# One PSUM tile per bank of attention scores, row maxima taken bank by bank, and the routing polynomial moved to VectorE from the third routing on

## The chip, the cores and the metric

One core of one Trainium2 chip runs the whole kernel; the other cores of the chip are idle. The metric is the time of one execution in microseconds (us), measured on the device. The kernel before takes 931.32 us, the median of 3 runs (929.89 to 932.29).

Names: PE is TensorE (PEld its weight load), DVE is VectorE, ACT is ScalarE, POOL is GpSimd and SP is SyncE, which here only issues DMAs. PSUM is the matmul result memory; it has 8 banks of 512 fp32 words per partition.

## The reference

Attention (batch 4, 8 heads, 768 positions, head dimension 64) in which a position sees the 96 positions up to itself and the first 8 of the sequence, with a linear distance bias; its output goes through a mixture of 8 experts, of which each of the 3072 tokens takes the best two by noisy logits.

```python
scores = scale * q @ k.T + bias;  scores = where(keep, scores, -1e9)
a = exp(scores - max(scores));  a = a / (sum(a) + 1e-9);  x = a @ v
noisy = x @ w_gate + log1p(exp(x @ w_noise)) * noise
top2 = argpartition(-noisy, 2)[:, :2]
top2_w = exp(l - max(l)) / (sum + 1e-9)          # l: the two noisy logits
for e in experts, k in range(2):                  # tokens whose k-th choice is e
    out[mask] += top2_w[mask, k, None] * (relu(x[mask] @ w1[e]) @ w2[e])
```

All matmuls of the experts are fp32, each done as three products of halves (hi*hi, lo*hi, hi*lo).

## The kernel before, in words

Each engine works through its own queue in the order in which the code issues instructions, with semaphore waits put in wherever two of them touch the same tile. No scheduler moves anything: the code order is the order.

**Attention** runs over 24 groups of 128 queries (`g`), two steps each, 48 steps `s` in all. A step handles two units `n` and `n+1`, where a unit is four score blocks laid out in one PSUM bank. The steps are software-pipelined. Step `s`, with `n = 2s`, issues in this order:

1. `trans(n)`: PE turns the probabilities of step `s` (L601, into `atb`);
2. `probs(n+2)`: ACT takes two exponentials of one bank (L572);
3. in odd steps `heads_out` (L632, ACT) and `gate_s2` (DVE); in even steps `gate_l2` (L216, ACT) and `gate_x2` (L203, DVE);
4. `evac(n)`: ACT copies the turned probabilities out of PSUM (L607);
5. `probs(n+3)`: ACT, two exponentials of the other bank; `total(n+2)`: POOL sums the probabilities (L582, L584); `total2(n-2)`: DVE (L589);
6. some *ticks* of the routing, then `product(n+4)`: PE writes the next two units' scores (L544) and biases (L550) into two of the three banks of `scb`, unit `n` into bank `n % 3`; then `top(n+4)`: DVE takes the maxima of both banks at once (L562) and scales them (L563);
7. `attend(n-2)` (L625), and the gate's matmuls (`gate_l` L211, `gate_x` L199 in odd steps, `gate_s` L220 in even ones).

In step `s`, `product(n+4)` fills banks `(n+4) % 3` and `(n+5) % 3`. The second of these is the bank that `probs(n+2)` reads in the same step; `probs(n+3)` reads the third bank, which `product(n+4)` doesn't touch. But `scb` is one tile of three banks.

**Routing** (`route(r)`) is a generator for each of five segments of groups, `SEG`. A tick advances every active routing by one step, and the routing with `r == CLOSE` (2) by two. It holds small DVE and ACT operations, a polynomial for log1p (L255 to L269) on POOL, the search for the two best (L276, L278, DVE), prefix sums by matmul (L308 to L312, PE), and two scatters a group into the table `tbl` in DRAM (L333, POOL). Routings 0 to 2 finish within attention; the first expert's first four tiles of tokens are gathered from their entries (L344, L159), and turned by PE (L176) into the banks of `scb`. Routing 3 ends, and routing 4 runs, while PE does the first expert's first matmuls (L851), by a fixed list of steps:

```python
steps_of = [10, 60], [0, 23, 0, 0, 100]
```

The routing's matmuls therefore stand in PE's queue between the first expert's matmuls. When routing 4 has written its entries, the rest of the table is read (L937) and the tokens of the other tiles are gathered.

**The experts** are 571 us of nearly gapless matmuls (L851, L884, L894).

Of the kernel before, what the change touches and what calls it, by code (L numbers as in the profile page):

```python
# [10 lines left out]
F32 = mybir.dt.float32  # L11
# [9 lines left out]
P = 128  # L21
# [9 lines left out]
def tile_local_global_attention_then_moe(  # L31
# [204 lines left out]
    def route(r):  # L236
# [17 lines left out]
        po_ = nc.gpsimd  # L254
        po_.tensor_mul(u, u, t)  # L255
        po_.tensor_mul(t, u, u)
        yield
        po_.tensor_scalar(p, t, SP_C[7], SP_C[6], op0=OP.mult, op1=OP.add)
        for j in range(5, -1, -1):
            po_.tensor_mul(p, p, t)  # L260
            po_.tensor_scalar(p, p, SP_C[j], None, op0=OP.add)  # L261
            if j % 2 == 0:
                yield
        po_.tensor_mul(p, p, u)
        po_.tensor_scalar(u, n, 0.0, None, op0=OP.max)
        yield
        po_.tensor_add(p, p, u)
        po_.tensor_mul(p, p, noise_s[:, a:z])
        po_.tensor_add(ny, p, l[:, :, :E])  # L269
        for _ in range(4):  # L270
            yield
# [83 lines left out]
    with ExitStack() as actx:  # L355
# [36 lines left out]
        if windowed:  # L392
# [67 lines left out]
            scb = ap.tile([P, 3, 512], F32, name="scb")  # L460
# [47 lines left out]
        def tick():  # L508
            beat[0] += 1
            active[:] = [(x, r) for x, r in active if next(x, 0) is None and (r != CLOSE or next(x, 0) is None)]  # L510
# [9 lines left out]
        def product(n):  # L520
# [5 lines left out]
            for x in range(2):  # L526
                SC[n + x] = scb[:, (n + x) % 3, :2 * w].rearrange("p (y w) -> p y w", y=2)
# [27 lines left out]
        def top(n):  # L555

            g, u, b, i = geo(n)
            w = WIN if i else P
            j = sorted([n % 3, (n + 1) % 3])
            ps = scb[:, j[0]:j[1] + 1:j[1] - j[0], :2 * w].rearrange("p x (y w) -> p x y w", y=2)  # L560
            t = aw.tile([P, 2, 2], F32, name="mx", bufs=4)
            nc.vector.tensor_reduce(t, ps[:, :, :, :P + NS] if i else ps, op=OP.max, axis=AX.X, negate=True)  # L562
            nc.vector.tensor_scalar(t, t, scale, None, op0=OP.mult)  # L563
            for x in range(2):
                MX[n + x] = t[:, j.index((n + x) % 3)]
# [174 lines left out]
        else:  # L740
# [36 lines left out]
            for s in range(NPR + 1):  # L777
# [18 lines left out]
                if s:  # L796
                    total2(n - 2)
                    if not odd:
                        sums(s // 2 - 1)
                if s + 2 < NPR:  # L800
                    ticks(3 if odd else 1)
# [14 lines left out]
                if s >= NPR - 1:  # L816
                    for t in (2 * (s - NPR + 1), 2 * (s - NPR + 1) + 1):
                        turn(0, t, scb[:, t % 3])
# [262 lines left out]
```

## Time and profile before

| | us |
|---|---|
| median of 3 runs | 931.32 |
| the profiled execution | 933.77 |
| its span, first to last instruction | 932.0 |
| attention, up to the last scores (269.92) | 270 |
| from there to the first gapless expert matmuls (361) | 91 |
| the experts after that | 571 |

| engine | busy us | share | instructions |
|---|---|---|---|
| PE | 781.2 | 84% | 7399 |
| DVE | 328.5 | 35% | 783 |
| ACT | 321.1 | 34% | 688 |
| POOL | 306.9 | 33% | 407 |

Engines work side by side, so busy times don't add up to the span. A share over the whole span mixes the attention, in which PE waits in every step, with the experts, in which it doesn't. The waits of a step have to be read from that step.

### The profile page before, as it was taken

To read this page: it belongs to the slowest core of one execution; us is meant where nothing else is said; L and a number is where in the kernel's file an instruction comes from. 1 tells how busy PE (TensorE), PEld (TensorE's weight loads), DVE (VectorE), ACT (ScalarE), POOL (GpSimd) and SP (SyncE) were. 2 spreads that over 40 slices of the span, in tenths; PEclk is the share of its full clock that TensorE was granted. 3 is DMA by queue.
4 is the path that set the end of the run, shared out by engine and by line. 5 is a ranking of instruction groups with operands and counts; after the bars stand their busy time and mean duration, and the time that the engine had idled before them with its cause. 6 is when DMAs were issued, how large, how long until landed. Compare 5 with 4: busy or idle time off the path is not lost.

```text
span 932.0 us, 17968 instructions
## 1 busy us (share of the span) xinstructions
PE 781.2 (84%) x7399; PEld 680.9 (73%) x7399; DVE 328.5 (35%) x783; ACT 321.1 (34%) x688; POOL 306.9 (33%) x407
## 2 busy tenths in 40 slices
PE   4566666565565398999999999999999999999995
PEld 3555555554554386989889899898898998988994
DVE  5343554444333241433234234224333323323400
ACT  2444454443432131333333233233333333333301
POOL 3222546646452755140231312313214124032013
PEclk9998998878896798999999999999999999999998
DMA  9158455443103275252533444435335344342014
GB/s 286 52 179 275 132 169 145 145 155 117 44 26 106 75 149 110 71 148 91 104 87 97 90 114 114 90 110 126 77 77 126 105 94 117 100 83 51 4 15 61
DMA packets 61253, 100.54 MB, mean 108 GB/s; under 512 B 11674, under 2 KB 20122, under 8 KB 61162
## 3 DMA queue, kind: packets, MB, share of 16 engines
q1 hardware_dynamic: 45930, 72.62, 25.0%
q0 software_dynamic: 15232, 26.68, 16.1%
q8 instruction: 60, 0.98, 0.4%
q14 instruction: 31, 0.25, 0.1%
HBM read 71.03 MB, written 28.24 MB: 107 GB/s over the span
## 4 chain that ended last, share of the span: by engine, by line
PE 50%; issue 22%; POOL 10%; ACT 8%; DVE 4%; DMA 3%; another core or an unknown queue 1%; POOLq 0%; ACTq 0%; DVEq 0%
PE av L884 10%; PE at L851 9%; PE sc L851 9%; PE av L894 7%; PE scb L544 4%; ACT a L572 4%; ACT at L607 3%; POOL out_dram L869 3%; PE otb L625 2%; PE atb L601 2%; DVE mx L562 2%; POOL tbl L333 2%; POOL xg L159 1%; DMA tbl<-ent,sli 1%; POOL p L261 1%
## 5 line engine op out<-in xcount | busy, mean ns | idle before, releaser
L544 PE MATMUL scb<-ks,qbuf 64*64 64x128 f32 (+1 forms) x1408 | 48.5, 283 | 102.9 <-ACT a L572 97.5
L869 POOL DMA_INDIRECT out_dram<-y,tba x28 | 44.4, 1587 | 257.3 <-ACT y L868 257.3
L544 PEld LDWEIGHTS scb<-ks,qbuf 64*64 64x64 f32 x1408 | 40.9, 155 | 114.7 <-ACT a L572 109.4
L572 ACT ACTIVATE a<-scb,mx 128x192 f32<-128x192 f32 (+1 forms) x192 | 68.7, 415 | 127.2 <-DVE mx L563 84.7
L884 PE MATMUL av<-w2h,hh 128*128 128x512 f32 x256 | 103.2, 403 | 0.0
L884 PE MATMUL av<-w2h,hl 128*128 128x512 f32 x256 | 102.0, 398 | 0.0
L884 PE MATMUL av<-w2l,hh 128*128 128x512 f32 x256 | 101.6, 397 | 0.0
L851 PE MATMUL at<-xh,w1h 128*128 128x512 f32 (+1 forms) x256 | 91.5, 357 | 1.5 <-DVE xl L179 1.5
L144 DVE TENSOR_TENSOR w1l<-raw,w1h 128x512 fp32r<-128x512 f32 x56 | 38.3, 689 | 148.1 <-ACT w1h L143 148.1
L851 PE MATMUL sc<-xh,w1h 128*128 128x512 f32 (+1 forms) x256 | 89.9, 351 | 0.0
L851 PE MATMUL at<-xh,w1l 128*128 128x512 f32 (+1 forms) x256 | 89.8, 351 | 0.0
L851 PE MATMUL at<-xl,w1h 128*128 128x512 f32 (+1 forms) x256 | 89.8, 351 | 0.0
L851 PE MATMUL sc<-xl,w1h 128*128 128x512 f32 (+1 forms) x256 | 88.4, 345 | 0.0
L851 PE MATMUL sc<-xh,w1l 128*128 128x512 f32 (+1 forms) x256 | 88.4, 345 | 0.0
L869 POOL DMA_INDIRECT out_dram<-y,tbb x24 | 38.1, 1589 | 148.6 <-ACT y L868 148.3
L894 PE MATMUL av<-hh,w2h 128*128 128x300 f32 x256 | 78.9, 308 | 0.0
L582 POOL TENSOR_TENSOR tot<-a 128x256 f32<-128x256 f32 x48 | 35.0, 730 | 129.1 <-ACT a L572 129.1
L894 PE MATMUL av<-hl,w2h 128*128 128x300 f32 x256 | 77.1, 301 | 0.0
L894 PE MATMUL av<-hh,w2l 128*128 128x300 f32 x256 | 77.0, 301 | 0.0
L562 DVE TENSOR_REDUCE mx<-scb 128x4 f32<-128x672 f32 (+1 forms) x48 | 39.8, 829 | 100.3 <-PE scb L550 98.5
L862 DVE SCALAR_TENSOR_TENSOR hl<-sc,hh 128x300 fp32r<-128x300 f32 (+1 forms) x62 | 35.8, 577 | 103.8 <-ACT hh L861 99.4
L861 ACT ACTIVATE hh<-sc 128x300 fp32r<-128x300 f32 (+1 forms) x62 | 31.4, 507 | 99.4 <-PE sc L851 98.2
(154 smaller groups left out, 1659.0 us busy)
## 6 DMA issues: line engine op xcount, KB each, us to landing
raw<-in_w SPq DMA_DIRECT2D x32, 1024.0 KB
out_dram<-zero SPq DMA_DIRECT2D x14, 512.0 KB
qbuf<-in_q SPq DMA_DIRECT2D x24, 256.0 KB
vs<-in_v SPq DMA_DIRECT2D x24, 256.0 KB
xd<-xr SPq DMA_DIRECT2D x24, 256.0 KB
ks<-in_k SPq DMA_DIRECT2D x8, 560.0 KB
vp<-in_vb SPq DMA_DIRECT2D x40, 80.0 KB
ks<-in_k SPq DMA_DIRECT2D x6, 432.0 KB
```

The costliest lines, as they stand in the source:

```text
L144: eng.tensor_sub(lo, t, hi.bitcast(F32))
L544: nc.tensor.matmul(SC[n + x][s * Q:(s + 1) * Q, y, c:c + wc], qs[b, j][r, 2 * i0 + s, u + y], m, start=y == 0 and full, stop=False, tile_p ...
L562: nc.vector.tensor_reduce(t, ps[:, :, :, :P + NS] if i else ps, op=OP.max, axis=AX.X, negate=True)
L572: nc.scalar.activation(A[n][:, y, :3 if i else 2, n % 2], ps[:, y].rearrange("p (c t) -> p c t", t=Q), AF.Exp, bias=mx[:, y:y + 1], scale= ...
L582: nc.gpsimd.tensor_add(t, a[:, :, 0], a[:, :, 1])
L607: nc.scalar.activation(AT[n][:, :, :m].rearrange("p y c t -> p y (c t)"), atb[:, :, :m * P], AF.Copy)
L851: nc.tensor.matmul(ps, w[:, k, fs], x[c][:, k], start=n == 0, stop=n == 3 * KC - 1)
L861: nc.scalar.activation(hh[c][:, f], ps, AF.Relu)
L862: nc.vector.scalar_tensor_tensor(hl[c][:, f], ps, 0.0, hh[c][:, f].bitcast(F32), op0=OP.max, op1=OP.subtract)
L869: ins = nc.gpsimd.indirect_dma_start(out=out, out_offset=bass.IndirectOffsetOnAxis(ap=r[:, 0:1], axis=0), in_=y, in_offset=None, bounds_ch ...
L884: nc.tensor.matmul(ps, x[0][:, f, cols], w[:, f], start=n == 0, stop=n == 3 * FC - 1)
L894: nc.tensor.matmul(ps, w[:, f, cols], x[1][:, f], start=n == 0, stop=n == 3 * FC - 1)
```

## The change

Three edits. The three banks of `scb` become three tiles, and `top` reduces each bank by an instruction of its own. The polynomial stays on POOL for routings 0 and 1, with a yield after every second operation instead of every sixth; from routing 2 on it is on DVE in 13 instructions, each with a yield. Ticks advance every routing from 2 on by two steps instead of only routing 2, and there are ticks in the last two steps too.

```diff
-        po_ = nc.gpsimd
-        po_.tensor_mul(u, u, t)
...
-            po_.tensor_scalar(p, p, SP_C[j], None, op0=OP.add)
-            if j % 2 == 0:
+        if r < CLOSE:
+            nc.gpsimd.tensor_mul(u, u, t)
...
+                nc.gpsimd.tensor_mul(p, p, t)
+                nc.gpsimd.tensor_scalar(p, p, SP_C[j], None, op0=OP.add)
                 yield
...
+        else:
+            nc.vector.tensor_mul(u, u, t)
+            yield
...
+            for j in range(6, 0, -1):
+                nc.vector.scalar_tensor_tensor(p, p, SP_C[j], t, op0=OP.add, op1=OP.mult)
+                yield
...
+            nc.vector.tensor_add(ny, p, l[:, :, :E])
             yield
...
-            scb = ap.tile([P, 3, 512], F32, name="scb")
+            scb = [ap.tile([P, 512], F32, name=f"sc{j}") for j in range(3)]
...
-            active[:] = [(x, r) for x, r in active if next(x, 0) is None and (r != CLOSE or next(x, 0) is None)]
+            active[:] = [(x, r) for x, r in active if next(x, 0) is None and (r < CLOSE or next(x, 0) is None)]
...
-                SC[n + x] = scb[:, (n + x) % 3, :2 * w].rearrange("p (y w) -> p y w", y=2)
+                SC[n + x] = scb[(n + x) % 3][:, :2 * w].rearrange("p (y w) -> p y w", y=2)
...
-            nc.vector.tensor_reduce(t, ps[:, :, :, :P + NS] if i else ps, op=OP.max, axis=AX.X, negate=True)
+            for x in range(2):
+                nc.vector.tensor_reduce(t[:, x], SC[n + x][:, :, :P + NS] if i else SC[n + x], op=OP.max, axis=AX.X,
+                                        negate=True)
...
+                ticks(4 if s + 2 >= NPR else 3 if odd else 1)
                 if s + 2 < NPR:
-                    ticks(3 if odd else 1)
...
-                        turn(0, t, scb[:, t % 3])
+                        turn(0, t, scb[t % 3])
```

The order in PE's queue within a step is the same; its waits are not. Before, in a step of the attention (L601 transposes, L544 scores, square brackets for the semaphores that an instruction waits on):

```order
L601 MATMUL atb<-ident,a_220 128x128 x6
L544 MATMUL scb<-ks,qbuf_110 64x128 [waits DMAHW7_49,DVE_49,Activation_49]
L544 MATMUL scb<-ks,qbuf_110 64x128 x3
L544 MATMUL scb<-ks,qbuf_110 64x40 x4
L544 MATMUL scb<-ks,qbuf_110 64x128 x4
```

The first score waits for ACT, and everything behind it in the queue with it. In the changed kernel, where L616 are the transposes, L561 the scores, and `sc_223` to `sc_225` the three banks:

```order
L616 MATMUL atb<-ident,a_221 128x128 [waits Activation_49]
L616 MATMUL atb<-ident,a_221 128x128 x2
L616 MATMUL atb<-ident,a_221 128x128 [waits Activation_49]
L616 MATMUL atb<-ident,a_221 128x128 x2
L561 MATMUL sc_223<-ks,qbuf_110 64x128
L561 MATMUL sc_224<-ks,qbuf_110 64x128 [waits DVE_49,Activation_49]
L561 MATMUL sc_223<-ks,qbuf_110 64x128
```

Before, the one wait on ACT stood ahead of both banks' scores and also covered the transposes of the next step. Now the transposes have waits of their own, the first bank's scores have none, and the second bank's have one, on the exponentials that read that bank.

On POOL, at the end of attention and the start of the experts, this stood before (L333 scatters, then routing 4's polynomial L255 to L269, then `hl`, the low half of an expert's activations, L859):

```order
L333 DMA tbl<-ent_4070,sli_4134 25600x2 x8
L255 TENSOR_TENSOR u_4160<-u_4160,t_4161 128x32
L256 TENSOR_TENSOR t_4161<-u_4160 128x32
...
L268 TENSOR_TENSOR p_4162<-p_4162,noise_s 128x32
L269 TENSOR_TENSOR ny_4163<-p_4162,LG 128x32
L859 TENSOR_TENSOR hl_4045<-h,hh_4043 128x512
L144 TENSOR_TENSOR w2l<-raw,w2h 128x512
L859 TENSOR_TENSOR hl_4045<-h,hh_4043 128x512 x2
L333 DMA tbl<-ent_4211,sli_4293 25600x2 x8
```

And now, with the scatters on L350 and `hl` on L874:

```order
L159 DMA xg<-xd,tb_88 128x512 x4
L350 DMA tbl<-ent_3950,sli_4023 25600x2 x7
L874 TENSOR_TENSOR hl_4143<-h,hh_4141 128x512
L144 TENSOR_TENSOR w2l<-raw,w2h 128x512
L350 DMA tbl<-ent_3950,sli_4023 25600x2
L874 TENSOR_TENSOR hl_4143<-h,hh_4141 128x512
L144 TENSOR_TENSOR w2l<-raw,w2h 128x512
L874 TENSOR_TENSOR hl_4143<-h,hh_4141 128x512 x2
L350 DMA tbl<-ent_4296,sli_4322 25600x2 x8
```

The polynomial is gone from POOL here, and seven of routing 3's eight scatters stand ahead of the first expert's `hl`.

On DVE, routing 4's polynomial now stands between the reciprocal and the search for the two best (L293, L295):

```order
L272 TENSOR_TENSOR u_4196<-u_4196,t_4197 128x32
L274 TENSOR_TENSOR t_4197<-u_4196 128x32
L276 TENSOR_SCALAR p_4198<-t_4197 128x32
L279 SCALAR_TENSOR_TENSOR p_4198<-p_4198,t_4197 128x32 x6
L281 SCALAR_TENSOR_TENSOR p_4198<-p_4198,u_4196 128x32
L283 SCALAR_TENSOR_TENSOR p_4198<-LG,p_4198 128x32
L285 TENSOR_TENSOR p_4198<-p_4198,noise_s 128x32
L287 TENSOR_TENSOR ny_4199<-p_4198,LG 128x32
L293 MAX m_4218<-ny_4199 128x8 x2
```

Before, the polynomial was twenty instructions on POOL, and DVE's queue went from the reciprocal (L252) straight to a wait for POOL.

## Rows read from the trace of the kernel before

**Rows 1.** The profile's page: busy time, and the span in 40 slices of 23.3 us (PE's busy tenths, PE's granted clock in tenths of full speed).

```profile
PE 781.2 (84%) x7399; PEld 680.9 (73%) x7399; DVE 328.5 (35%) x783; ACT 321.1 (34%) x688; POOL 306.9 (33%) x407
...
PE   4566666565565398999999999999999999999995
...
PEclk9998998878896798999999999999999999999998
```

**Rows 2.** Stretches of the span: length, busy us of each engine (instructions), granted clock, DMA share, GB/s. 14.02, 91.17 and 269.92 are the starts of the scores of units 4, 34 and 94, the last: 15 and 30 steps apart.

```profile
14.02:91.17 77.15, 48.00 (x1134) 40.29 (x1135) 32.19 (x84) 34.93 (x88) 19.33 (x34) 0.93 0.58 190
91.17:269.92 178.75, 108.38 (x2554) 92.53 (x2554) 80.03 (x277) 77.07 (x195) 94.18 (x156) 0.86 0.40 122
361.00:932.00 571.00, 559.73 (x3200) 498.11 (x3198) 179.24 (x304) 184.72 (x354) 139.19 (x104) 0.99 0.39 91
```

**Rows 3.** Who waited for whom between 20 and 276 us: us in total, times, longest.

```profile
PE scb L544 <- ACT a L572: 91.4, 44, 4.9
ACT a L572 <- DVE mx L563: 76.4, 30, 3.2
DVE m L276 <- POOL ny L269: 14.2, 3, 5.6
```

**Rows 4.** The timeline of one step with no routing in it: start, us, engine and line; in brackets the idle time before, and what ended it.

```profile
86.24 0.88 PE L544 MATMUL scb<-ks,qbuf 64*64 64x128 f32 x32 [1.58 <-ACT a L572]
...
87.40 0.86 DVE L562 TENSOR_REDUCE mx<-scb 128x4 f32<-128x672 f32 x1 [2.21 <-PE scb L550]
...
88.29 0.17 DVE L563 TENSOR_SCALAR mx<-mx 128x4 f32<-128x4 f32 x1
...
88.58 0.73 ACT L572 ACTIVATE a<-scb,mx 128x192 f32<-128x192 f32 x2 [2.39 <-DVE mx L563]
...
89.20 0.60 ACT L632 ACTIVATE ot<-otb 128x512 f32<-128x512 f32 x1
89.68 0.82 ACT L607 ACTIVATE at<-atb 128x768 f32<-128x768 f32 x1
90.37 0.75 ACT L572 ACTIVATE a<-scb,mx 128x192 f32<-128x192 f32 x2
91.17 1.52 PE L544 MATMUL scb<-ks,qbuf 64*64 64x128 f32 x32 [2.54 <-ACT a L572]
...
93.12 0.86 DVE L562 TENSOR_REDUCE mx<-scb 128x4 f32<-128x672 f32 x1 [3.74 <-PE scb L550]
...
95.15 0.82 PE L601 MATMUL atb<-ident,a 128*128 128x128 f32 x6
```

**Rows 5.** PE's part of an odd step at full clock, the longer of the two kinds, from the same view.

```profile
269.92 0.88 PE L544 MATMUL scb<-ks,qbuf 64*64 64x128 f32 x32 [1.58 <-ACT a L572]
...
272.42 0.82 PE L601 MATMUL atb<-ident,a 128*128 128x128 f32 x6
```

**Rows 6.** POOL up to 345 us, and two groups of DVE up to 360 us, by line and shape: busy us, mean ns, idle time before.

```profile
L333 POOL DMA_INDIRECT tbl<-ent,sli x48 | 48.7, 1016 | 13.0 <-issue 10.7 <-DVE m L276 0.9 <-DVE sli L328 0.3
L582 POOL TENSOR_TENSOR tot<-a 128x256 f32<-128x256 f32 x48 | 35.0, 730 | 129.1 <-ACT a L572 129.1
L584 POOL TENSOR_TENSOR tot<-tot,a 128x160 f32<-128x160 f32 x40 | 20.9, 522 | 3.1
...
L563 DVE TENSOR_SCALAR mx<-mx 128x4 f32<-128x4 f32 x48 | 11.2, 234 | 1.7
L562 DVE TENSOR_REDUCE mx<-scb 128x4 f32<-128x512 f32 x8 | 5.5, 692 | 15.6 <-PE scb L550 15.6
L244 DVE SCALAR_TENSOR_TENSOR u<-LG 128x40 f32<-128x40 f32 x2 | 0.3, 148 | 0.0
```

**Rows 7.** Two small DVE instructions, each with the POOL instruction that ran at that time, from the timelines of both engines.

```profile
129.89 1.27 POOL L144 TENSOR_TENSOR w1l<-raw,w1h 128x512 fp32r<-128x512 f32 x1
130.20 0.98 DVE L563 TENSOR_SCALAR mx<-mx 128x4 f32<-128x4 f32 x1
302.64 1.31 POOL L859 TENSOR_TENSOR hl<-h,hh 128x512 fp32r<-128x512 f32 x1 [17.36 <-ACT hh L858]
302.69 1.31 DVE L244 SCALAR_TENSOR_TENSOR u<-LG 128x32 f32<-128x32 f32 x1
```

**Rows 8.** After the last scores: the timelines of PE, POOL and DVE.

```profile
282.59 1.11 PE L176 MATMUL scb<-ident,xg 128*128 128x128 f32 x4 [5.42 <-DMA xg<-xd,tb]
285.19 1.08 PE L176 MATMUL scb<-ident,xg 128*128 128x128 f32 x4 [1.49 <-DVE xl L179]
292.61 1.11 PE L176 MATMUL scb<-ident,xg 128*128 128x128 f32 x4 [1.41 <-DVE xl L179]
305.26 0.35 DVE L252 RECIPROCAL t<-t 128x32 f32<-128x32 f32 x1
315.42 0.27 POOL L255 TENSOR_TENSOR u<-u,t 128x32 f32<-128x32 f32 x1
322.03 0.25 POOL L269 TENSOR_TENSOR ny<-p,LG 128x32 f32<-128x32 f32 x1
322.32 0.24 DVE L276 MAX8 m<-ny 128x8 f32<-128x8 f32 x2 [16.70 <-POOL ny L269]
324.12 0.20 PE L308 MATMUL lg<-ohs,upper 128*128 128x8 bf16 x2 [14.33 <-DVE ohs L294]
357.62 0.93 PE L176 MATMUL m<-ident,xg 100*128 100x100 f32 x4 [2.59 <-DMA xg<-xd,tbb]
```

More of the change, by code (lines that the diff above doesn't have):

```diff
@@ L253, in route @@
         yield
-        po_ = nc.gpsimd
-        po_.tensor_mul(u, u, t)
[L256 to L260, printed above, removed]
-            po_.tensor_scalar(p, p, SP_C[j], None, op0=OP.add)
-            if j % 2 == 0:
-                yield
[L264 to L270, printed above, removed]
+        if r < CLOSE:
+            nc.gpsimd.tensor_mul(u, u, t)
+            nc.gpsimd.tensor_mul(t, u, u)
+            yield
+            nc.gpsimd.tensor_scalar(p, t, SP_C[7], SP_C[6], op0=OP.mult, op1=OP.add)
+            for j in range(5, -1, -1):
+                nc.gpsimd.tensor_mul(p, p, t)
+                nc.gpsimd.tensor_scalar(p, p, SP_C[j], None, op0=OP.add)
+                yield
+            nc.gpsimd.tensor_mul(p, p, u)
+            nc.gpsimd.tensor_scalar(u, n, 0.0, None, op0=OP.max)
+            yield
+            nc.gpsimd.tensor_add(p, p, u)
+            nc.gpsimd.tensor_mul(p, p, noise_s[:, a:z])
+            nc.gpsimd.tensor_add(ny, p, l[:, :, :E])
+            for _ in range(3):
+                yield
+        else:
+            nc.vector.tensor_mul(u, u, t)
+            yield
+            nc.vector.tensor_mul(t, u, u)
+            yield
+            nc.vector.tensor_scalar(p, t, SP_C[7], None, op0=OP.mult)
+            yield
+            for j in range(6, 0, -1):
+                nc.vector.scalar_tensor_tensor(p, p, SP_C[j], t, op0=OP.add, op1=OP.mult)
+                yield
+            nc.vector.scalar_tensor_tensor(p, p, SP_C[0], u, op0=OP.add, op1=OP.mult)
+            yield
+            nc.vector.scalar_tensor_tensor(p, n, 0.0, p, op0=OP.max, op1=OP.add)
+            yield
+            nc.vector.tensor_mul(p, p, noise_s[:, a:z])
+            yield
+            nc.vector.tensor_add(ny, p, l[:, :, :E])
             yield
@@ L557, in top @@
             g, u, b, i = geo(n)
-            w = WIN if i else P
-            j = sorted([n % 3, (n + 1) % 3])
-            ps = scb[:, j[0]:j[1] + 1:j[1] - j[0], :2 * w].rearrange("p x (y w) -> p x y w", y=2)
             t = aw.tile([P, 2, 2], F32, name="mx", bufs=4)
-            nc.vector.tensor_reduce(t, ps[:, :, :, :P + NS] if i else ps, op=OP.max, axis=AX.X, negate=True)
+            for x in range(2):
+                nc.vector.tensor_reduce(t[:, x], SC[n + x][:, :, :P + NS] if i else SC[n + x], op=OP.max, axis=AX.X,
+                                        negate=True)
+                MX[n + x] = t[:, x]
             nc.vector.tensor_scalar(t, t, scale, None, op0=OP.mult)
-            for x in range(2):
-                MX[n + x] = t[:, j.index((n + x) % 3)]
         def probs(n):
```

## The prediction

> **What bounds the kernel now.** I read the page first [rows 1]: PE is busy 84% of the span, but its tenths stand at 5 to 6 in slices 2 to 12, the attention, and at 9 behind them. A table of stretches comes next [rows 2]: from 361 us to the end PE works 559.7 of 571 us at a granted clock of 0.99, so the experts are bound by PE's own work and the change leaves that alone. In the attention the busiest engine, PE, works 48.0 of 77.15 us and 108.4 of 178.75, so there something else sets the pace. The waits [rows 3] name a ring: PE's scores wait 91.4 us for ACT's exponentials, ACT waits 76.4 us for the scaled maxima, and the maxima wait for the scores. The timeline of one step [rows 4] shows it link by link. The exponentials `probs(n+2)` run 88.58 to 89.31, then ACT does `ot`, the evacuation and the other bank's exponentials `probs(n+3)` (90.37 to 91.12); .05 us later, at 91.17, PE starts the scores. Thus both pairs of exponentials, the evacuation and `ot` stand in series with scores, maxima and scale: 86.24 to 91.17, 4.93 us a step.
>
> Over long stretches a step takes 77.15 / 15 = 5.14 us up to 91.17 and 178.75 / 30 = 5.96 us from there to 269.92, where the routings run [rows 2]. The rest, 270 to 361, is a chain of gathers, turns and routing 4 with PE often idle [rows 8].
>
> **The change, part by part.** The sums are made against the profiled execution's 933.77 us; the median of the runs, 931.32, is 2.45 lower, and I take that off at the end.
>
> *Three tiles for the three banks.* The second bank's scores now wait only for `probs(n+2)`, the first pair of the step, and the first bank's for a pair of the step before. The ring becomes: pair .73, start .05; start of scores to start of maxima 87.40 - 86.24 = 1.16; maxima; 88.58 less the maxima's end at 88.26 = .32 for the scale and the way to ACT [rows 4]. The maxima are now two instructions. One of 672 columns takes .86 and one of 512 .69 [rows 6], so a column costs .17 / 160 us and one of 336 comes to about .50, two to 1.00 instead of .86. Sum: .78 + 1.16 + 1.00 + .32 = 3.26 us. What is late next is not far behind: PE's own part of an odd step is 272.42 + .82 - 269.92 = 3.3 us [rows 5], and ACT's is .73 + .60 + .82 + .75 = 2.9 [rows 4]. With a PE of 3.3 and a ring of 3.3 that meet only on average, and with the .2 by which the steps of before exceeded their clean ring (5.14 against 4.93), I take 3.8 us for the quiet steps; 3.35 and 4.3 are the ends, the latter since the scores can run at the lower clock, where the way from scores to maxima is 93.12 - 91.17 = 1.95 and not 1.16 [rows 4]. **Term A**: 77.15 - 15 x 3.8 = 20, from 27 down to 12. The data for it have to keep up: the stretch moves 190 GB/s at a DMA share of .58 [rows 2], which becomes .58 x 77.15 / 57 = .79. That is under full, and I charge nothing; without that cover the stretch can't be shorter than .58 x 77.15 = 45 us, below my 57.
>
> *The thirty steps with routings* have the same ring and more beside it. What lengthened them by .82 us (5.96 against 5.14) is the routings' work in the queues of DVE and ACT, POOL's work and a clock of 0.86 against 0.93 [rows 2]. That part doesn't shrink with the ring, and the routing work now falls into a shorter time. I add 1.0 to 3.5, the midpoint of the ring with its locks and the 3.8 above without its .2 or .3: 4.5 us a step. **Term B**: 178.75 - 30 x 4.5 = 44, with 3.75 (66) and 5.2 (23) as ends. POOL keeps up at that: it works 94.18 us there, 3.14 a step, of which routing 2's polynomial goes away [rows 2].
>
> *The polynomial on DVE.* In routings 2 to 4 twenty POOL instructions, 322.28 - 315.42 = 6.9 us for 32 columns [rows 8], become 13 on DVE. No row has such a run on DVE. A two-input DVE operation of 40 columns takes .148 [rows 6], so 13 take 1.9, and with .02 between them 2.2. The other bound is each waiting out a POOL operation: the scale L563, usually .17, took .98 while a weight split of 1.27 ran, and L244 1.31 [rows 7]; at .6 for each, about half such a split, the 13 take 7.8. I take 2.2 in the open and lay it in attention beside PE's wait, for DVE works 80 of 178.75 us there. DVE's queue loses a wait in return: MAX stood 14.2 us for POOL in three places, with the scales behind it [rows 3]; that is part of why B may reach its better end.
>
> The Trainium skill, page "SBUF — State Buffer", section "Who interferes with whom", says that DVE and GpSimd share one pair of ports under an exclusive lock, which an instruction of DVE with two SBUF inputs or in a two-port mode also needs. The trace agrees: L563 of .17 became .98 beside a POOL split [rows 4, 7]. By that rule the move to DVE isn't free of POOL, and the last rival below is what it would cost at worst.
>
> *The transition.* Three parts. PE waits 5.42 us for the gathered tokens before 282.59, which were issued behind routing 3's polynomial on POOL; with that on DVE I take back 3, from 1 to 5.4. The turns wait 1.49 and 1.41 us for the copy of the bank before only since the banks were one tile: 2.9 back, 0 at worst. PE is idle 14.33 us, from 309.79 to 324.12, for routing 4 [rows 8]. That routing's reciprocal ends at 305.61; its polynomial could only start on POOL behind eight scatters, at 315.42, and MAX ran at 322.32, 1.80 before PE. With DVE: 305.61 + 2.2 + 1.80 = 309.6, the very time at which PE falls idle. I leave 3 of the 14.33 for a POOL lock and a late PE signal, so 11 back; at .6 an instruction it is 305.61 + 7.8 + 1.80 = 315.2, so 324.1 - 315.2 = 9 at worst. The 2.59 us before the `tbb` gather at 357.62 [rows 8] hang on routing 4's entries, which now come some 14 us earlier while PE comes 11 earlier; I count 1. **Term C**: 3 + 2.9 + 11 + 1 = 18, from 10 to 22.
>
> Nothing is taken for the ticks in the last two steps and the finer yields: they move work that is in the terms already.
>
> Sum: 20 + 44 + 18 = 82; 933.77 - 82 = 851.8 profiled, less 2.45: 849.
>
> **The rivals.**
>
> *POOL sets the pace with the routings.* A scatter is 1.02, the totals .73 + .52 a unit [rows 6], a weight split 1.27 [rows 7]. A step with three scatters, one unit's totals beyond the usual and a split comes to 3 x 1.02 + 1.25 + 1.27 = 5.6; one without a split 4.3. If such steps and their locks make the mean 5.0 in the thirty, B is 29 and the time 933.77 - 20 - 29 - 18 - 2.45 = 864. For it: POOL's 94 us there against 19 in the quiet stretch. Against it: its mean of 3.14 a step, and a scale that waits at most one POOL instruction.
>
> *PE at its lower clock bounds the steps.* In the step from 91.17 the scores run 1.52 and the step's last PE work, L601, ends at 95.97: 4.8 us, against 3.3 at the full level [rows 4, 5]. If attention stays at the 1.2 GHz level, A becomes 77.15 - 15 x 4.8 = 5 and, with .4 for routings, B 178.75 - 30 x 5.2 = 23; with C at 15 that is 43, thus 888. For it: a granted clock of .86. Against: a ring with fewer gaps keeps PE busier, and PE at .98 share has .99 [rows 1, 2].
>
> The Trainium skill, page "TensorE: Matmul & The Clock Gate", Part 1, has it that the slow level is the default and activity lifts it. The rows agree as far as they go: the gapless experts run at .99, the gappy attention at .93 and .86 [rows 2]; by that rule the shorter ring would raise the clock, so this rival gets little.
>
> *The split frees nothing in the ring*, since another wait takes its place at once (the transposes, which need both pairs of exponentials, ahead of the scores in PE's queue). Then only C comes: 933.77 - 18 - 2.45 = 913. For it: L601 now waits for ACT itself. Against: L601 concerns the exponentials of the step before, which are over by then.
>
> *The lock makes it slower.* Some 180 DVE instructions up to routing 4's end can meet the lock: 48 scales, 39 of the polynomial, and about 94 of the normalization and the routings. If they meet a POOL instruction more often, in queues that the scale stands in, and each loses time on the ring, the gain of 82 is gone at 82 / 180 = .45 us each; from there on it decides. At .6 each, half a split, it is 108, thus 933.77 - 82 + 108 - 2.45 = 957. For it: 1.31 us for an L244 of .15 [rows 6, 7]. Against: the 48 scales have a mean of .234 [rows 6], .06 over the usual one, and POOL sees less work, not more.
>
> **How the numbers follow.** My forecast .68, POOL as the pace .18, the lower clock .06, nothing in the ring .05, the lock .03. The range: all terms at their good ends, 27 + 66 + 22 = 115, give 816; all at their bad ends, 12 + 23 + 10 = 45, give 886. I take 818 to 890: it holds the first two rivals and leaves out the last two and some of the forecast's own edges. About .3%, 2.8 us, is what a measurement of this kernel can tell from no change. Every case but the last is faster by far more: faster .95, same .02 for mixtures of the last two, slower .03.
>
> **What would show it.** Right: the scores' starts 3.5 to 4.5 us apart; next to no wait of the scores for `a`; `MAX` waiting for POOL's `ny` only in routings 0 and 1; PE idle under 5 us ahead of routing 4's `ohs` matmul; the experts' 571 us as they were. Wrong: a mean of L563 well over .4 (the lock), a wait of the exponentials or totals for POOL (the first rival), scores of 1.5 us throughout (the clock), an interval near 5 (nothing freed), or experts that take longer because the weights or gathers behind the faster part come late.

## The result and the profile after

The changed kernel takes 861.61 us, the median of 4 runs (859.50 to 862.50), beside 931.81 for the kernel before (4 runs): a ratio of 0.9241 (95% interval 0.9212 to 0.9271; the ratios are the recorded ones and differ a little from the quotients of the medians, here 0.9247). The prediction was 849 us, from 818 to 890. The profiled execution took 859.50 us, its span 857.7.

The page of the changed kernel, the lines that answer to [rows 1]: busy time, then PE's busy tenths and granted clock in 40 slices of 21.4 us.

```profile
PE 781.3 (91%) x7399; PEld 676.1 (79%) x7399; DVE 347.5 (41%) x870; ACT 320.5 (37%) x688; POOL 289.8 (34%) x347
...
PE   6988785787579899999999999999999999999994
...
PEclk9999998979589999999999999999999999999998
```

PE does the same 781 us of work. Its tenths in the attention rose from 5 and 6 to 7 and 8; the weakest slices of this part are now the 7th (129 to 150 us), in which a routing stops the steps, and the 11th (214 to 236), the first turns, where the clock falls to .5.

Stretches of the changed kernel, with the columns of [rows 2]. 13.42, 65.89 and 202.67 are the starts of the biases (L567) of the same units as there, 233.84 is the first expert matmul. The biases serve as the mark, since a step's scores are now split by a wait.

```profile
13.42:65.89 52.47, 46.79 (x1140) 38.42 (x1139) 34.56 (x100) 33.59 (x87) 19.29 (x34) 1.00 0.79 257
65.89:202.67 136.78, 108.08 (x2563) 88.35 (x2559) 89.87 (x321) 76.42 (x196) 87.75 (x136) 0.91 0.58 170
202.67:233.84 31.17, 16.89 (x251) 12.51 (x243) 14.26 (x61) 7.92 (x18) 14.10 (x16) 0.67 0.23 69
233.84:857.70 623.86, 603.60 (x3403) 532.83 (x3403) 200.44 (x364) 198.40 (x379) 161.62 (x123) 0.99 0.41 94
```

The fifteen quiet steps take 52.47 / 15 = 3.50 us, and PE is busy for 89% of them at a clock of 1.00. The thirty steps with routings take 136.78 / 30 = 4.56. In the trace of before the same marks stand at 15.32, 92.47 and 270.61, and the first expert matmul at 295.22. The last two of its stretches:

```profile
270.61:295.22 24.61, 12.56 (x230) 9.51 (x223) 7.67 (x18) 6.67 (x14) 11.16 (x28) 0.74 0.28 87
295.22:932.00 636.78, 607.37 (x3417) 535.23 (x3417) 200.27 (x380) 198.14 (x380) 174.52 (x150) 0.97 0.40 92
```

So the four stretches gave 1.9 us (up to the first mark), 24.7, 41.4, and then 24.6 - 31.2 = -6.6 and 636.8 - 623.9 = 12.9: together 74.3, the difference of the two spans.

The waits of the attention, as in [rows 3]:

```profile
ACT a L587 <- DVE mx L580: 30.6, 26, 2.1
...
DVE m L293 <- POOL ny L268: 12.5, 2, 8.0
...
PE sc L561 <- ACT a L587: 8.4, 17, 1.3
```

PE's wait for the exponentials went from 91.4 us to 8.4, ACT's for the maxima from 76.4 to 30.6. Of DVE's waits for POOL's polynomial two are left, with 12.5 of 14.2 us. A quiet step in the timeline, to be read beside [rows 4]:

```profile
62.07 0.88 PE L561 MATMUL sc<-ks,qbuf 64*64 64x128 f32 x32
...
62.94 0.72 ACT L587 ACTIVATE a<-sc,mx 128x192 f32<-128x192 f32 x2
63.21 0.92 DVE L577 TENSOR_REDUCE mx<-sc 128x2 f32<-128x336 f32 x2 [0.17 <-PE sc L567]
...
64.17 0.33 DVE L580 TENSOR_SCALAR mx<-mx 128x4 f32<-128x4 f32 x1
...
64.61 0.73 ACT L587 ACTIVATE a<-sc,mx 128x192 f32<-128x192 f32 x2 [0.95 <-DVE mx L580]
...
65.40 0.67 PE L561 MATMUL sc<-ks,qbuf 64*64 64x128 f32 x21 [0.58 <-ACT a L587]
...
65.71 0.82 ACT L622 ACTIVATE at<-atb 128x768 f32<-128x768 f32 x1
...
66.40 0.75 ACT L587 ACTIVATE a<-sc,mx 128x192 f32<-128x192 f32 x2
```

The scores at 65.40 follow the first pair of exponentials (64.61 to 65.34) by .06 us, and the evacuation and the second pair (65.71, 66.40) lie beside them. From scores to maxima it is 63.21 - 62.07 = 1.14 us, and two reductions take .92 against .86 for one.

The longest of the thirty steps runs from 128.2 to 141.5 us:

```profile
134.37 0.27 POOL L268 TENSOR_TENSOR ny<-p,LG 128x40 f32<-128x40 f32 x1
134.67 0.24 DVE L293 MAX8 m<-ny 128x8 f32<-128x8 f32 x2 [8.02 <-POOL ny L268]
...
135.78 0.67 DVE L203 TENSOR_TENSOR xr<-otb,rd 128x512 f32<-128x512 f32 x1
...
136.51 0.92 PE L640 MATMUL otb<-at,vs 64*64 64x128 f32 x16 [7.92 <-DVE xr L203]
...
138.24 0.91 DVE L577 TENSOR_REDUCE mx<-sc 128x2 f32<-128x336 f32 x2
...
140.18 0.73 ACT L587 ACTIVATE a<-sc,mx 128x192 f32<-128x192 f32 x2 [1.69 <-DVE mx L580]
```

MAX of routing 1 waits 8.02 us at the head of DVE's queue for the last of the polynomial's instructions on POOL, where scatters and sums stand between them. The normalization `xr`, the maxima, and by them PE and ACT all wait behind it. The second such step (83.8 to 92.6) belongs to routing 0.

The transition, places where PE was slow or PE and ACT idle first, then routing 4's polynomial on DVE and what POOL did at that time:

```profile
214.84 1.67 PE L211 MATMUL lg<-ot,wgn 128*32 128x128 f32 x8
...
220.19 0.59 PE L176 MATMUL sc<-ident,xg 128*128 128x128 f32 x2 [0.31 <-issue]
226.00 1.08 ACT L178 ACTIVATE xh<-sc 128x512 fp32r<-128x512 f32 x2 [12.15 <-remote]
228.67 0.92 PE L640 MATMUL otb<-at,vs 64*64 64x128 f32 x16 [7.89 <-DVE xr L203]
...
251.91 0.19 PE L325 MATMUL lg<-ohs,upper 128*128 128x8 bf16 x2 [5.79 <-DVE ohs L311]
```

```profile
242.54 6.63 DVE L279 SCALAR_TENSOR_TENSOR p<-p,t 128x32 f32<-128x32 f32 x6
...
243.16 1.31 POOL L874 TENSOR_TENSOR hl<-h,hh 128x512 fp32r<-128x512 f32 x1
244.42 1.32 POOL L144 TENSOR_TENSOR w2l<-raw,w2h 128x512 fp32r<-128x512 f32 x1
245.66 1.30 POOL L874 TENSOR_TENSOR hl<-h,hh 128x512 fp32r<-128x512 f32 x1
```

PE's idle time ahead of routing 4's prefix sums fell from 14.33 us [rows 8] to 5.79. Six instructions of the polynomial took 6.63 us beside POOL's splits. And ACT copied the first turned tokens at 226.00, 5.2 us after PE's last transposes of them (220.78). PE itself was slow before that: from the products at 211.74 to the end of these transposes 9.0 us passed, with idle places that the profile puts down to `issue`. In the second trace of the same kernel (below) the same work takes 4.2 (208.82 to 213.03), L211's eight matmuls .65 and not 1.67.

### The profile page after: what moved, and what is told of

Read it like the earlier page. It is cut to its first block, busy times and chain, and to the rows that moved or that the text cites. A ratio compares the mean times of both kernels' runs of the same rounds, so it can differ in the third digit from the quotient of the medians.

```text
span 857.7 us, 18060 instructions
## 1 busy us (share of the span) xinstructions
PE 781.3 (91%) x7399; PEld 676.1 (79%) x7399; DVE 347.5 (41%) x870; ACT 320.5 (37%) x688; POOL 289.8 (34%) x347
## 4 chain that ended last, share of the span: by engine, by line
PE 60%; issue 17%; POOL 8%; DVE 6%; DMA 3%; ACT 2%; another core or an unknown queue 2%; POOLq 0%; ACTq 0%; DVEq 0%
PE av L899 14%; PE at L866 12%; PE sc L866 12%; PE av L909 9%; PE sc L561 3%; PE otb L640 2%; POOL out_dram L884 2%; PE atb L616 2%; DVE mx L577 2%; ACT a L587 1%; POOL tbl L350 1%; DMA tbl<-ent,sli 1%; PE m L176 1%; PE sc L567 1%
## 5 line engine op out<-in xcount | busy, mean ns | idle before, releaser
L587 ACT ACTIVATE a<-sc,mx 128x192 f32<-128x192 f32 (+1 forms) x192 | 68.9, 417 | 65.3 <-DVE mx L580 38.6
L561 PE MATMUL sc<-ks,qbuf 64*64 64x40 f32 (+1 forms) x1408 | 57.4, 268 | 19.7 <-ACT a L587 11.0
L640 PE MATMUL otb<-at,vs 64*64 64x64 f32 (+1 forms) x1088 | 49.4, 260 | 27.1 <-DVE xr L203 22.0
L561 PEld LDWEIGHTS sc<-ks,qbuf 64*64 64x64 f32 x1408 | 43.4, 143 | 34.8 <-issue 17.1
L640 PEld LDWEIGHTS otb<-at,vs 64*64 64x64 f32 x1088 | 42.9, 147 | 29.7 <-DVE xr L203 15.1
```

Source lines behind the costliest of these rows:

```text
L561: nc.tensor.matmul(SC[n + x][s * Q:(s + 1) * Q, y, c:c + wc], qs[b, j][r, 2 * i0 + s, u + y], m, start=y == 0 and full, stop=False, tile_p ...
L587: nc.scalar.activation(A[n][:, y, :3 if i else 2, n % 2], ps[:, y].rearrange("p (c t) -> p c t", t=Q), AF.Exp, bias=mx[:, y:y + 1], scale= ...
L640: nc.tensor.matmul(otb[y * Q:(y + 1) * Q, x, u // 2 * P:(u // 2 + 1) * P][:, cols], t[r, h * D:(h + 1) * D], a[r, y, c, cols], start=j == ...
```

## The experiments

They were run in three sittings of four kernels, each sitting on a chip of its own (a "place" below) and beside runs of the kernel before: 923.64, 923.67 and 934.38 us, against 931.81 in the first measurement. The changed kernel itself was run again in the second sitting alone and took 844.00. So the first two sittings, in which the kernel before took the same time, are compared with 923.6 and 844.0, the third with 931.8 and 861.6, and across those two pairs ratios are used. Even a ratio isn't free of the place: the changed kernel's own is 0.9241 in the one and 0.9148 in the other.

**One part at a time.** The first kernel has only the three tiles and the maxima bank by bank:

```diff
-            scb = ap.tile([P, 3, 512], F32, name="scb")
+            scb = [ap.tile([P, 512], F32, name=f"sc{j}") for j in range(3)]
...
-            nc.vector.tensor_reduce(t, ps[:, :, :, :P + NS] if i else ps, op=OP.max, axis=AX.X, negate=True)
...
+                nc.vector.tensor_reduce(t[:, x], SC[n + x][:, :, :P + NS] if i else SC[n + x], op=OP.max, axis=AX.X,
+                                        negate=True)
```

> The kernel before with three score tiles and bank-by-bank maxima alone; polynomial, yields and ticks as before. Theory (the tiles are nearly the whole gain, by the ring of the steps): the quiet fifteen steps fall from 5.14 to about 3.5 us (-25), the thirty with routings to about 4.7 (-38), the two waits between the turns go (-3): about 866 us. Rival (the two edits need each other, since POOL's polynomial holds the maximum search in every routing once the ring is short): the quiet steps fall the same, the thirty stay above 5.2 (-22), about 881 us or more.

Measured: 861.72 us, ratio 0.9328 (0.9307 to 0.9349), -61.9 us. Its stretches by the same marks, and its wait for the polynomial:

```profile
13.41:65.25 51.84, 47.75 (x1141) 39.33 (x1139) 34.47 (x100) 33.29 (x87) 19.30 (x34) 1.00 0.78 256
65.25:199.19 133.94, 102.41 (x2563) 86.09 (x2559) 86.46 (x307) 75.64 (x196) 91.27 (x152) 0.89 0.59 174
```

```profile
DVE m L276 <- POOL ny L269: 24.7, 3, 10.6
```

The theory held and the rival fell: quiet steps 3.46 us, the others 133.94 / 30 = 4.46. But the rival's mechanism is there: three of the thirty steps take 9.5, 13.8 and 14.1 us, those in which MAX waits for POOL, and the other 27 take (133.9 - 37.4) / 27 = 3.6, hardly more than the quiet ones. In the trace of before the same three steps take 5.8, 8.9 and 11.9 us, with waits of 14.2, and the others 5.6: there the waits lengthened them by 9.8 us, here by 26.7.

The second kernel has the routing edits on the single score tile:

```diff
-        po_ = nc.gpsimd
+        if r < CLOSE:
...
+        else:
+            nc.vector.tensor_mul(u, u, t)
...
-            active[:] = [(x, r) for x, r in active if next(x, 0) is None and (r != CLOSE or next(x, 0) is None)]
+            active[:] = [(x, r) for x, r in active if next(x, 0) is None and (r < CLOSE or next(x, 0) is None)]
...
+                ticks(4 if s + 2 >= NPR else 3 if odd else 1)
```

> The kernel before with the routing edits alone (polynomial, yields, ticks), one score tile, one maximum for both banks. Theory: steps without routings stay at 4.9 us; MAX loses one wait for POOL of about 5 us; the 14.3 us of idle PE ahead of routing 4's prefix sums fall to 3 to 6: in all -10 to -16, 916 to 922 us. Rival (the extra DVE instructions and their lock eat that up in the attention): 930 us or more, with longer steps between 91 and 270 us.

Measured: 910.84 us, ratio 0.9862 (0.9829 to 0.9895), -12.8 us; quiet steps 5.13 us, 5.70 us of idle PE ahead of routing 4. As expected, but for one thing: MAX waits for POOL nowhere in the attention of this kernel, not even in routings 0 and 1. The two parts, both from the first sitting, come to -74.7 beside -79.7 for both together in the second.

**Where the polynomial costs.** VectorE takes it in all five routings:

```diff
-        if r < CLOSE:
+        if r < 0:
             nc.gpsimd.tensor_mul(u, u, t)
```

> The changed kernel with the polynomial on VectorE in all five routings. Theory (the two steps of 8.8 and 13.2 us are DVE's queue standing behind MAX, which waits 4.5 and 8.0 us for POOL): both waits go, the two steps fall to 5 to 6 us, and 26 more DVE instructions cost 2 to 4 us: 850 to 855 us. Rival (the shared port: the 26 instructions take .34 or more each in the ring, and L580 gets longer): within 2 us of 861.6, or above.

Measured: 830.63 us, ratio 0.8989 (0.8970 to 0.9007), -13.4 against the changed kernel's 844.0. The thirty steps:

```profile
65.80:185.35 119.55, 99.21 (x2563) 81.86 (x2559) 100.91 (x345) 75.49 (x196) 75.43 (x94) 0.99 0.67 195
```

They fall from 4.46 (133.81 / 30 in the changed kernel's second trace) to 3.98. The two long steps of 9.0 and 15.8 us take 4.5 and 3.8, the steps ahead of them, to which MAX moves, 5.0 and 6.2 instead of 3.6 and 3.3. The waits for POOL were 14.8 us in that second trace, and 13.4 came back in spite of 26 more DVE instructions. The gain is larger than the 7 to 12 I had put down from a yardstick of 861.6; beside 844.0, measured on another chip with the same time of the kernel before, it is the size of the wait. The clock rose too, from 0.89 to 0.99, and PE's busy time in these steps fell from 105.4 to 99.2 us; what the wait gave and what the clock gave isn't separated.

**The late copy.** Routing 3's scatters are moved behind the first expert's `hl`:

```diff
+        for _ in range(30 if r == 3 else 0):
+            yield
         for i in range(w):
             for j in range(2):
```

> The changed kernel with routing 3's eight scatters moved behind the first expert's first hl (30 empty steps of the routing ahead of them). In the changed kernel 32.4 us pass from the start of the last scores to the first expert matmul, 25.3 before; ACT starts the first turn's copy 5.2 us after PE's last transposes, while seven scatters run back to back on POOL. Theory (a run of scatters holds up the signal from PE): without them there the copy starts within .5 us of the transposes, the stretch falls to 26 to 28 us, and of that 2 to 5 us reach the end, as the scatters now stand behind hl: 856 to 860 us. Rival (ACT was late for another reason): the stretch stays at 31 to 33, the time within 2 us of 861.6 or above.

Measured: 849.57 us, ratio 0.9191 (0.9170 to 0.9213): 5.6 us slower than the changed kernel in the second sitting. The stretch did fall to 22.4 us, but so it does without the edit, as the yardstick showed:

> The changed kernel once more, as the yardstick for the other runs and for one wait. Time: ratio to before .92 to .93. In its first profile ACT's copy of the first turn started at 226.00, 5.2 us after PE's last transposes, beside a run of seven scatters; with VectorE doing every polynomial the same run of scatters stood there and the copy came in time. If the late copy belongs to this program, the stretch from the last scores' biases to the first expert matmul is again about 31 us; if it was a thing of that one execution, it is 22 to 25 and the whole time is some 6 us shorter.

Measured: 844.00 us, ratio 0.9148 (0.9116 to 0.9181). Its stretches:

```profile
13.41:64.01 50.60, 45.82 (x1140) 37.81 (x1139) 34.38 (x100) 33.19 (x87) 19.30 (x34) 0.97 0.78 252
64.01:197.82 133.81, 105.43 (x2563) 87.78 (x2559) 92.40 (x319) 76.19 (x196) 86.47 (x134) 0.89 0.59 178
197.82:220.22 22.40, 13.71 (x250) 11.29 (x243) 15.20 (x63) 7.93 (x18) 14.76 (x17) 0.77 0.33 96
220.22:841.20 620.98, 602.20 (x3403) 531.87 (x3403) 200.38 (x364) 197.98 (x379) 162.69 (x124) 0.99 0.39 94
```

From the last biases to the first expert matmul it is 22.40 us, not 31.17, with the same instructions in the same queues. In the kernel with VectorE in all routings, too, a scatter runs while the copy comes in time:

```profile
198.75 1.39 PE L176 MATMUL sc<-ident,xg 128*128 128x128 f32 x8
199.16 1.02 POOL L350 DMA_INDIRECT tbl<-ent,sli  x1 [0.30 <-issue]
199.74 1.08 ACT L178 ACTIVATE xh<-sc 128x512 fp32r<-128x512 f32 x2 [2.99 <-PE sc L176]
```

So my theory that a run of scatters is enough to hold up PE's signal falls. What the scatters' move did show lies in routing 4. Two rows of DVE and of PE with the scatters held back:

```profile
232.42 1.32 DVE L279 SCALAR_TENSOR_TENSOR p<-p,t 128x32 f32<-128x32 f32 x6
...
236.24 0.19 DVE L311 TENSOR_TENSOR ohs<-oh,oh 128x32 bf16<-128x32 f32 x1
```

```profile
236.48 0.19 PE L325 MATMUL lg<-ohs,upper 128*128 128x8 bf16 x2 [0.44 <-DVE ohs L311]
...
275.04 0.93 PE L176 MATMUL m<-ident,xg 100*128 100x100 f32 x4 [8.18 <-DMA xg<-xd,tbb]
```

Beside scatters instead of splits the six instructions take 1.32 us, not 6.63, and PE idles .44 ahead of the prefix sums, not 5.8. But routing 4's own scatters and all behind them come later, and PE waits 8.18 us for the second gather. With both edits the same happens:

> Polynomial on VectorE in all routings and routing 3's scatters held back behind the first hl, together. If the two gains add up, 4 us below the kernel with VectorE in all routings (.899 of before), at .894 to .896. If the late copy doesn't exist there anyway (its stretch from the last biases to the first expert matmul was 21.9 us), holding the scatters back only makes the second gather later, by the 8.2 us of wait seen with the scatters held, of which some 3 reach the end: .899 to .903.

Measured: 835.70 us, ratio 0.9045 (0.9023 to 0.9067): 5.1 slower than without the held scatters, a bit beyond what the second theory allowed. The gains don't add.

**What the ring is worth.** Each bank's maxima are scaled behind their own reduction:

```diff
-            t = aw.tile([P, 2, 2], F32, name="mx", bufs=4)
             for x in range(2):
-                nc.vector.tensor_reduce(t[:, x], SC[n + x][:, :, :P + NS] if i else SC[n + x], op=OP.max, axis=AX.X,
+                t = aw.tile([P, 2], F32, name=f"mx{x}", bufs=4)
+                nc.vector.tensor_reduce(t, SC[n + x][:, :, :P + NS] if i else SC[n + x], op=OP.max, axis=AX.X,
                                         negate=True)
-                MX[n + x] = t[:, x]
-            nc.vector.tensor_scalar(t, t, scale, None, op0=OP.mult)
+                nc.vector.tensor_scalar(t, t, scale, None, op0=OP.mult)
+                MX[n + x] = t
```

> The changed kernel with each bank's maxima scaled by an instruction of its own, right behind its reduction, into a tile of its own. Theory (the ring bounds the steps): the first exponentials of a step start one reduction (.46 us) earlier, less the price of a second scale; the quiet steps fall from 3.5 to 3.3, where PE's own work bounds them, the others by .2 to .3: -6 to -12 us against the changed kernel. Rival (DVE's small SBUF instructions pay for the shared port): 48 more scales at .3 us each stand in DVE's queue and the time is the same or up to 8 us longer.

Measured: 834.17 us, ratio 0.9042 (0.9001 to 0.9083), -9.8. Quiet steps 48.65 / 15 = 3.24 us against 3.37 (second trace; 3.50 in the first), the thirty 126.95 / 30 = 4.23 against 4.46. The theory held: the ring still sets the pace wherever a reduction taken off it shows, and 48 more scales, with a mean of .30, are paid for.

**What the lock costs.** Each DVE instruction of the polynomial is issued twice:

```diff
+                nc.vector.scalar_tensor_tensor(dup, p, SP_C[j], t, op0=OP.add, op1=OP.mult)
                 nc.vector.scalar_tensor_tensor(p, p, SP_C[j], t, op0=OP.add, op1=OP.mult)
```

> The changed kernel with each of the 13 VectorE instructions of the polynomial issued twice in routings 2 to 4, the first of the two into a tile that nobody reads: 39 more. Theory (they lie beside other waits in attention and cost their own .2 in routing 4's chain): 13 x .2 = 2.6 there and 0 to 4 in attention, +3 to +7 us against the changed kernel. Rival (each meets the lock, .5 us or more): +15 to +20.

Measured: 850.21 us, ratio 0.9212 (0.9188 to 0.9235), +6.2 for 39 instructions: .16 us each. PE's idle time ahead of routing 4 went from 5.78 to 8.18, 2.4 for 13. The theory held; an added instruction doesn't meet a lock of its own each time. Where one does, though, it is dear. One instruction of this kernel, and POOL beside it:

```profile
232.61 4.37 DVE L279 TENSOR_SCALAR dup<-t 128x32 f32<-128x32 f32 x1
```

```profile
233.14 1.31 POOL L883 TENSOR_TENSOR hl<-h,hh 128x512 fp32r<-128x512 f32 x1
234.40 1.31 POOL L144 TENSOR_TENSOR w2l<-raw,w2h 128x512 fp32r<-128x512 f32 x1
235.66 1.29 POOL L883 TENSOR_TENSOR hl<-h,hh 128x512 fp32r<-128x512 f32 x1
```

**Is POOL the pace?** Two kernels of the third sitting, one without POOL's second sum of a unit (the denominators then lack the first positions of the sequence), one with both sums made twice:

```diff
-            if i:
-                nc.gpsimd.tensor_add(t[:, :, :, :NS], t[:, :, :, :NS], a[:, :, 2, :, :NS])
```

> The changed kernel without POOL's second sum of a unit (the first positions of the sequence are missing from the denominators): 40 POOL instructions of .52, 21 us of POOL's 106 busy us in the attention. Theory (POOL has slack and only the scales that meet it pay): 0 to -5 us against the changed kernel. Rival (POOL sets the pace of the steps with routings): -10 to -15.

Measured: 863.63 us, ratio 0.9234 (0.9194 to 0.9275), beside the changed kernel's 0.9241: no difference that can be told. The 10 to 15 us of the rival are excluded; the thirty steps take 139.1 / 30 = 4.64 us. A gain of a few us could hide, though. MAX's two waits are 8.5 us here and not 12.5, while the maxima's waits that no engine of the trace explains are 8.3 and not 5.0.

```diff
             t = aw.tile([P, 2, 2, Q], F32, name="tot", bufs=3)
+            td = aw.tile([P, 2, 2, Q], F32, name="totdup", bufs=1)
+            nc.gpsimd.tensor_add(td, a[:, :, 0], a[:, :, 1])
+            if i:
+                nc.gpsimd.tensor_add(td[:, :, :, :NS], td[:, :, :, :NS], a[:, :, 2, :, :NS])
```

> The changed kernel with both sums of a unit made twice on POOL, once into a tile that nobody reads: 56 us more of POOL work in the attention, 1.25 a unit of about 3.5 to 4.5 us. Theory (slack; the price is more meetings of scales and sums at the shared port): L580's mean from .30 to .40 and +5 to +12 us against the changed kernel, quiet steps under 3.7. Rival (POOL near its limit in the thirty steps): these rise from 4.5 to over 5.2, +20 us or more.

Measured: 874.55 us, ratio 0.9354 (0.9321 to 0.9388), +.0113 of 934, about 11 us. The size was as the theory had it, the reason not. L580's mean rose only to .32. The quiet steps take 3.68 us against 3.50, 2.7 in all; the thirty take 4.99 against 4.56, 12.8 in all, and 12.2 of that is MAX: the polynomials of routings 0 and 1, now queued behind more sums, make it wait 24.7 us and not 12.5.

```profile
DVE m L293 <- POOL ny L268: 24.7, 2, 15.8
```

So of 56 us more of POOL work little is paid for by itself; the time went through the one place where DVE waits for POOL.

**Both gains together, and the kernel before once more.**

> Polynomial on VectorE in all routings and each bank's maxima scaled by themselves, together. Against the changed kernel in the same place the one gave -13.4 us and the other -9.8. Theory (one frees the thirty steps of a wait for POOL, the other shortens the ring in all 48): most of both, -19 to -23, 821 to 826 us, .889 to .894 of before. Rival (both live on the same slack of DVE's queue): not under 829.

Measured: 847.26 us, ratio 0.9083 (0.9042 to 0.9125) in the third sitting, where the changed kernel's 0.9241 is the yardstick: -.0158, about 15 us. That is under the 19 to 23 of the theory. Its quiet steps take 3.25 us, as with the scaling alone, its thirty 127.3 / 30 = 4.24, and in these DVE is busy for 104.1 us. Up to the last biases it is 13.9 us ahead of the changed kernel's first trace (188.76 against 202.67); alone, in the other place, the two edits were 12.5 and 9.5 ahead of its second. That both gains draw on the same queue fits this, but isn't shown, since the places differ. Against the changed kernel in its own place it stands at .9083 / .9241 = .983, and VectorE in all routings alone at .8989 / .9148 = .983; which is better can't be told. Both beat the kernel before and the changed one.

> The kernel before once more, for a profile beside those of the experiments. In the first measurement it took 931.8 us, beside the experiments 923.6. Its first trace has 13.3 us of waits in the attention for PE signals that no engine of the trace explains. If these make the difference, the thirty steps with routings are about 8 us shorter here (171 us) and those waits are gone, while the quiet steps stay at 5.1 us and the stretch from the last biases to the end at 661.

Measured once: 933.2 us, span 931.5. This sitting ran at the level of the first measurement and not at 923.6, so it says nothing of the other place. It still tells something: quiet steps 5.16 us, the thirty 176.1, the rest 662.7, and none of the unexplained waits of the first trace, at nearly the same time. So these waits aren't what separates 932 from 924; what does stays open. They were also less than the 13.3 us of my expectation: DVE's 7.5 and ACT's 5.8 lie side by side, at 248.47 and 262.62.

## Why the prediction was right, and which term of it was not

The forecast of 849 us lies between the two times of the changed kernel, 861.6 and 844.0, so how near it comes is in part the doing of the place. Its terms against the first trace:

| term | forecast us | measured us |
|---|---|---|
| up to the first mark | 0 | 1.9 |
| A, fifteen quiet steps | 20 (12 to 27) | 24.7 |
| B, thirty steps with routings | 44 (23 to 66) | 41.4 |
| C, transition and experts | 18 (10 to 22) | 6.3 |
| sum | 82 | 74.3 |

**Term A** was right by its mechanism. The ring closed at .06 us behind the first pair, the maxima take .92 (estimate 1.00), scores to maxima 1.14 (1.16). I had taken 3.8 us a step for a ring of 3.26 and a PE of 3.3 that meet only on average; the mean is 3.50, with the clock at 1.00 instead of 0.93. The kernel with only the tiles shows that the tiles alone do this, the one with two scales that the ring still sets the pace. The data kept up at a DMA share of .79, the figure worked out.

**Term B** came out at 4.56 us a step for a forecast of 4.5, but the step "I add 1.0" had the wrong picture. It spread the routings' work over all thirty steps. Two steps alone, 8.8 and 13.2 us, hold 22 - 7 = 15 of the 30 x 1.06 = 32 us above the quiet pace, and they are the two waits of MAX for POOL that the prediction had left standing in routings 0 and 1 and priced at nothing. With those polynomials on DVE the step is 3.98. The 14.2 us of such waits stood in [rows 3] all along: in the slow ring part of them was hidden, in the fast one each holds DVE's queue, and with it the ring. The tiles alone make them 24.7; the routing edits alone, in the slow ring, leave none (with them MAX comes eleven yields after the polynomial's start instead of nine; the loop of before yields after every fourth operation, not every sixth). So the two waits left are the short ring's.

**Term C** failed in the first measurement: 6.3 instead of 18. It has two halves. From the first expert matmul to the end 12.9 us came (15.8 in the second trace, beside the one of before from the first place) of the 11 + 1 forecast. There the step "305.61 + 2.2 + 1.80" was mis-sized: the polynomial took from 241.22 to 250.07, 8.85 us, above the 7.8 of the bound at .6 an instruction, and PE idles 5.79 us instead of 3. That the half still gave the forecast's sum goes with the clock: with the shorter pause PE idles 9.1 us less (29.4 to 20.3), and its matmuls take 3.8 us less in the same stretch (607.4 to 603.6 busy) at a granted clock of .99 instead of .97, which the prediction had not counted. The half from the last scores to the first expert matmul was to give 3 + 2.9; it lost 6.6, by PE's slow passage ahead of the turns (4.8 us more than in the second trace) and the late copy at 226.00 (5.2 us after the transposes), neither of which the prediction knew. In the second sitting, against the same trace of before, it gave 2.2: the waits of 5.42, 1.49 and 1.41 us are gone, as forecast, but PE then waits 4.04 and 2.26 us for `xr` in a DVE queue that holds routing 3's polynomial. A wait removed there was followed by another.

**The rivals.** POOL as the pace was forecast at 864, near the time measured, but by the wrong road: without 21 us of POOL's sums the time is the same, and the thirty steps took 4.56 and not 5.0. The lower clock fell, the clock rose to 1.00 in the quiet part. "Nothing in the ring" fell with PE's wait of 8.4 us. The lock on the ring is there, since the scale's mean went from .234 to .291 (.324 in the second trace), but that is 48 x .06 to .09 = 3 to 4 us against the break-even of .45 an instruction.

The Trainium skill, page "SBUF — State Buffer", section "Who interferes with whom", says that a DVE instruction with two SBUF inputs contends with a GpSimd instruction that reads SBUF, under an exclusive lock. The 6.63 us beside splits and the 1.32 us beside scatters for the same six instructions agree. My own sentence that a scale waits for at most one POOL instruction held for the scales, of which the longest took 1.09 us. The bound of .6 an instruction that I gave the polynomial had the same thought behind it and didn't hold: 4.37 us passed for one DVE instruction, through three POOL instructions in a row.

**What to look for** came as listed, with two exceptions: PE's idle time ahead of routing 4 is 5.8 and not under 5, and MAX's remaining waits, foreseen but unpriced, held the largest gain found here (13.4 us).

## What to carry to other kernels

A ring that passes through several engines is shortened by asking of each wait in it which instruction it needs and which it gets by sharing a tile; three tiles for three banks gave 62 of the 80 us here. When the ring is shorter, look again at every wait at the head of an in-order queue that the ring passes through: a wait of 4.5 to 8 us for a slow engine, once partly covered, then costs its full length, and a mean over the steps hides that two of them carry it. Moving such work to the engine that waits for it paid here even under a port lock, but beside a run of long instructions of the other engine it paid less: routing 4's polynomial took 8.85 us and not the 2.2 of my estimate, and PE's idle time ahead of it fell to 5.8 us and not to 3.

## What the runs showed of the hardware that I had not expected

A DVE instruction that was shut out by POOL wasn't let in between two POOL instructions that followed at once. In the second trace of the changed kernel one instruction of the polynomial, usually .19 us, took 4.49, until the third POOL instruction ended at 233.36:

```profile
228.92 4.49 DVE L279 SCALAR_TENSOR_TENSOR p<-p,t 128x32 f32<-128x32 f32 x1
```

```profile
229.55 1.31 POOL L874 TENSOR_TENSOR hl<-h,hh 128x512 fp32r<-128x512 f32 x1
230.81 1.31 POOL L144 TENSOR_TENSOR w2l<-raw,w2h 128x512 fp32r<-128x512 f32 x1
232.07 1.29 POOL L874 TENSOR_TENSOR hl<-h,hh 128x512 fp32r<-128x512 f32 x1
```

The DVE row begins .6 us ahead of the first POOL row, while a scatter still runs, and what held it then the trace doesn't show. In seven other traces one instruction of routing 4's polynomial took 4.46 to 4.50 us beside the same three. Scatters alone don't shut it out: beside them, in the kernel with the scatters held back, the same instructions took .2 us.

One kernel with the same instructions took 861.6 us in one place and 844.0 in another, while the kernel before took 931.8 and 923.6. Of the 16.5 us between the spans of its two traces, 8.8 lie between the last scores and the first expert matmul, where PE was slow ahead of the turns and its signal to ACT came late; the others are spread over the quiet steps (1.9), the thirty (3.0) and the experts (2.9). Where the kernel has scatters in it, that stretch was 31.2 us in the first measurement and 29.8 to 32.3 in three traces of the third sitting, against 21.3 to 22.4 in five traces of the first two. What holds PE and its signal up isn't shown, and whether holding the scatters back would pay in that other place wasn't tried.
